# Moving rows placed 320 bytes past the weights, modulo 512, in an attention and channel-mix kernel

## The chip, the cores and the metric

The kernel runs on one core of a Trainium2 chip. The metric is the device time of one execution in microseconds. The core has a TensorE (PE; its weight loads are listed as PEld), a VectorE (DVE), a ScalarE (ACT), a GpSimd (POOL) and a SyncE (SP) that issues the DMAs. SBUF is the working memory: 128 partitions, each with its own range of byte addresses. A tile takes the same bytes of every partition. PSUM holds what TensorE accumulates.

## The reference, cut to what matters

```python
scores = scale * np.matmul(q, k.transpose(0, 1, 3, 2)) - np.log(S)     # q, k, v: 8 x 12 x 448 x 64
attn = 1.0 / (1.0 + np.exp(-scores))
x = np.matmul(attn, v)                   # then heads side by side: 8 x 448 x 768
x_prev = ...                             # x, one token earlier
xk = mu_k * x + (1.0 - mu_k) * x_prev
xr = mu_r * x + (1.0 - mu_r) * x_prev
k = np.maximum(xk @ w_k, 0.0)            # w_k: 768 x 1024
v = k * k @ w_v                          # w_v: 1024 x 768
r = 1.0 / (1.0 + np.exp(-(xr @ w_r)))    # w_r: 768 x 768
return r * v
```

The attention has no softmax, only a sigmoid. Behind it stand three products with weights: `xr @ w_r` (stage 0), `xk @ w_k` (stage 1) and `k*k @ w_v` (stage 2).

## The kernel before, in words

**Attention.** 48 pairs of heads are worked off two pairs at a time. For each of 7 strips of 64 keys, line 333 computes scores, ScalarE applies the sigmoid (line 337), and line 346 multiplies by the values. One step of either kind is four matmuls of 64x64 weights, one for each quarter of TensorE's array. Operands are plain f32 in the tiles raw, vn and pf. VectorE mixes each token with the one before it (lines 361 and 362) and the results go to DRAM as xr_d and xk_d. Beside it, VectorE converts the 64-bit weights to f32.

**Stages.** Each of the three products is a two-by-two block product done with seven block products instead of eight, over four pairs of token blocks (the first pair has blocks of 256 tokens, the others of 512). The seven left factors, sums and differences of weight blocks, lie in `slots`, one slot each. Every factor is split into a high part rounded to the type f32r and a low part, the rest, so that one product is made of three: high by high, high by low, low by high. The right factors, the activations, are fetched into ysa, ysb and other tiles (`fetch`), combined there (`minus`, line 415), and split into high and low rows by `operand` (lines 427 and 428). The split rows go into the 24 units of rra and rrb, 12 each, taken round in turn by `take`. Line 551 in `multiply` issues all matmuls of the stages: 128x128 of a slot are loaded as weights, and one row of 512 f32r columns (256 in part of the first pair of blocks) moves through the array into PSUM tile xb or yb. Each matmul has its own weight load. `evacuate` and `out_block` empty xb and yb on ScalarE and VectorE.

**Order.** All instructions of a part are put into one order by `Plan`, a list scheduler with a cost for each operation (`mm` in line 197 prices a matmul at `n * (cols / 2.4 + 13.5)` ns), priorities and data dependences. It knows no addresses. The queues of the engines then run in that order, with waits on data.

**Places in SBUF.** Tiles of a pool lie one behind the other in the order in which they are made. The pool wp stands on the left, directly above the constants; the pools on the right (apool in the attention, kp in the stages, after apool is closed) end at the top of memory, so that a longer pool begins lower. In the program of before the tiles begin at these bytes of each partition:

| Tile | first byte | modulo 512 | length |
|---|---|---|---|
| slot0 to slot6 (weights) | 16672 to 90400 | 288 | 12288 each |
| rra (moving rows) | 102688 | 288 | 24576 |
| ysa, wraw, wbit, wexpo | 127264 to 162080 | 288 | multiples of 2048 |
| rrb (moving rows) | 167712 | 288 | 24576 |
| ysb, u2, cc, wc | 192288 to 227616 | 288 | multiples of 512 |

A block of 128 weights takes 512 bytes of a partition and a row of 512 takes 2048, so all blocks of weights and all rows of the stages begin at the same byte modulo 512 as the tiles. kp already ends with an unused tile, gap1, of 48 elements or 192 bytes.

Of the kernel before, what the change touches and what calls it, by code (L numbers as in the profile page):

```python
# [8 lines left out]
F32 = mybir.dt.float32  # L9
# [89 lines left out]
def attention_then_channel_mix(  # L99
# [17 lines left out]
    P = 128  # L117
# [41 lines left out]
    def ring(pool, name, bufs, shape, dtype):  # L159
        return [pool.tile(shape, dtype, name=f"{name}{i}") for i in range(bufs)]  # L160

    wp = ctx.enter_context(tc.tile_pool(name="wp", bufs=1, side="left"))
    att = ExitStack()
    slots = [wp.tile([P, 2 * WO], F32R, name=f"slot{g}") for g in range(7)]
    RU = 2 * NJH
    rra = wp.tile([P, 2 * RU, TB], F32R, name="rra")
    ysa = wp.tile([P, RU, TB], F32, name="ysa")
    wraw = wp.tile([P, 2, WP, 2], U32, name="wraw")
# [211 lines left out]
    def take(n):  # L380
        x = rr_n[0] if rr_n[0] + n <= 4 * RU else 0
        rr_n[0] = x + n
        names = [("rra", u) if u < 2 * RU else ("rrb", u - 2 * RU) for u in range(x, x + n)]
        return [big[name][:, u] for name, u in names], names
# [112 lines left out]
    kp = ctx.enter_context(tc.tile_pool(name="kp", bufs=1, side="right", reuse_waits="tile"))  # L497
    rrb = kp.tile([P, 2 * RU, TB], F32R, name="rrb")
    ysb = kp.tile([P, RU, TB], F32, name="ysb")
    big["rrb"], big["ysb"] = rrb, ysb  # L500
    u2 = ring(kp, "u2", 4, [P, TB], F32)
    cc = ring(kp, "cc", 5, [P, TB], F32)
    wc = ring(kp, "wc", 4, [P, WC], F32)
    kp.tile([P, 48], F32, name="gap1")
    pb = ctx.enter_context(tc.tile_pool(name="pb", bufs=1, space=PSUM, reuse_waits="tile"))
    yb = ring(pb, "yb", 4, [P, TB], F32)
    xb = ring(pb, "xb", 4, [P, TB], F32)
# [198 lines left out]
```

## Time and profile before

| | |
|---|---|
| median of 3 runs | 817.62 us (817.34 to 818.55) |
| the profiled execution | 817.73 us |
| its span, first to last instruction | 815.9 us |
| granted TensorE clock, mean | 0.999 |
| TensorE busy | 810.4 us, 5259 matmuls |
| VectorE busy | 595.5 us |
| ScalarE busy | 490.3 us |

The span is what the views of the profile cover; 1.8 us of the execution lie around it. The chain of waits follows the work that ended last back to the start. In the chain in order of time, a piece of TensorE is a number of matmuls back to back; its length by its count is their spacing. The mean duration of a matmul in the groups of instructions is longer than this spacing, because matmuls overlap.

### The profile page before, as it was taken

The page shows a single profiled execution, that of the slowest core. Times are in us where ns is not written, and L with a number is a line of the kernel's source. Part 1 is how long each engine was busy: PE and PEld are TensorE (multiplying, and loading weights), DVE is VectorE, ACT ScalarE, POOL GpSimd, SP SyncE. Part 2 cuts the span into 40 slices and gives each one's busy share as a digit, 9 for nine tenths or more (in the row PEclk, how much of TensorE's full clock was granted, in tenths as well). Part 3 has the DMA queues.
Part 4 walks back from the last instruction along what each step waited for, and adds up shares of the span by engine and source line. Part 5 has one row for each costly group of instructions (what it writes and reads, how often), then busy time and mean ns, then how long its engine had stood idle before and what let it go on. Part 6 is the DMA issues. An engine that isn't in the chain of part 4 may idle for free.

```text
span 815.9 us, 14820 instructions
## 1 busy us (share of the span) xinstructions
PE 810.4 (99%) x5259; PEld 568.1 (70%) x5259; DVE 595.5 (73%) x1120; ACT 490.3 (60%) x846; POOL 10.7 (1%) x100
## 2 busy tenths in 40 slices
PE   9999999999999999999999999999999999999998
PEld 4444444444445888888888888888888888888887
DVE  1999889787666999899983624566587495494675
ACT  5776766666566756456774855878695434333442
POOL 0000000000000000000000000000000000000000
PEclk9999999999999999999999999999999999999999
DMA  9888879998954775859885531724763565554442
GB/s 303 270 301 272 275 271 346 310 369 309 301 188 155 262 243 210 286 194 308 287 263 196 194 117 51 257 74 135 272 224 107 212 217 181 174 162 155 134 139 90
DMA packets 113881, 179.77 MB, mean 220 GB/s; under 512 B 14096, under 2 KB 78608, under 8 KB 112272
## 3 DMA queue, kind: packets, MB, share of 16 engines
q1 hardware_dynamic: 113520, 178.54, 65.1%
q8 instruction: 41, 0.67, 0.3%
q10 hardware_dynamic: 288, 0.30, 0.1%
q14 instruction: 32, 0.26, 0.1%
HBM read 109.06 MB, written 69.73 MB: 219 GB/s over the span
## 4 chain that ended last, share of the span: by engine, by line
PE 97%; DVE 2%; issue 1%; ACT 0%; DMA 0%; DVEq 0%
PE xb L551 38%; PE yb L551 28%; PE sc L333 16%; PE av L346 15%; DMA raw<-in_qk 0%; DVE rrb L428 0%; DVE xo L362 0%; DVE cc L604 0%; DVE xo L361 0%; DVE ysa L415 0%; DVE ysb L415 0%; DVE rra L428 0%; DVE cc L589 0%; ACT yb L666 0%; ACT cc L601 0%
## 5 line engine op out<-in xcount | busy, mean ns | idle before, releaser
L337 ACT ACTIVATE pf<-sc 128x896 f32<-128x896 f32 x168 | 153.9, 917 | 88.2 <-PE sc L333 88.1
L551 PE MATMUL xb<-rra,slot 128*128 128x512 f32 (+1 forms) x807 | 188.1, 381 | 0.1
L551 PEld LDWEIGHTS xb<-rra,slot 128*128 128x128 f32 x807 | 147.4, 188 | 30.3 <-issue 0.7
L333 PE MATMUL sc<-raw 64*64 64x448 f32 (+1 forms) x1360 | 157.5, 535 | 0.3 <-DMA raw<-in_qk 0.2
L346 PE MATMUL av<-pf,vn 64*64 64x448 f32 x1344 | 156.2, 536 | 0.0
L551 PE MATMUL xb<-rrb,slot 128*128 128x512 f32 (+1 forms) x645 | 149.7, 378 | 0.2 <-DVE cc L604 0.2
L551 PEld LDWEIGHTS xb<-rrb,slot 128*128 128x128 f32 x645 | 116.7, 188 | 23.3 <-DVE cc L604 0.4
L551 PE MATMUL yb<-rrb,slot 128*128 128x512 f32 (+1 forms) x547 | 127.1, 380 | 0.0
L551 PE MATMUL yb<-rra,slot 128*128 128x512 f32 (+1 forms) x546 | 126.1, 378 | 0.0
L551 PEld LDWEIGHTS yb<-rrb,slot 128*128 128x128 f32 x547 | 99.5, 188 | 19.6
L551 PEld LDWEIGHTS yb<-rra,slot 128*128 128x128 f32 x546 | 98.8, 188 | 19.3
L333 PEld LDWEIGHTS sc<-raw 64*64 64x64 f32 x1360 | 53.0, 134 | 75.1 <-issue 69.5
L346 PEld LDWEIGHTS av<-pf,vn 64*64 64x64 f32 x1344 | 51.4, 133 | 74.9 <-issue 74.2
L361 DVE TENSOR_SCALAR xo<-av,omr 128x447 f32<-128x447 f32 x48 | 32.5, 677 | 43.7 <-PE av L346 43.7
L428 DVE TENSOR_TENSOR rrb<-ysa,rrb 128x512 fp32r<-128x512 f32 (+1 forms) x61 | 36.4, 633 | 32.3 <-ACT rrb L427 29.3
L601 ACT COPY u<-yb 128x512 f32<-128x512 f32 x40 | 23.3, 586 | 54.5 <-PE yb L551 54.5
L428 DVE TENSOR_TENSOR rra<-ysa,rra 128x512 fp32r<-128x512 f32 (+1 forms) x71 | 40.0, 601 | 16.8 <-ACT rra L427 10.7
L427 ACT CAST rra<-ysa 128x512 fp32r<-128x512 f32 (+1 forms) x75 | 38.6, 554 | 12.0 <-PE xb L551 5.3
L601 ACT COPY cc<-yb 128x512 f32<-128x512 f32 (+1 forms) x49 | 26.3, 542 | 26.9 <-PE yb L551 22.9
L427 ACT CAST rrb<-ysa 128x512 fp32r<-128x512 f32 (+1 forms) x61 | 33.0, 577 | 15.4 <-PE xb L551 10.9
L604 DVE TENSOR_TENSOR cc<-xb,cc 128x512 f32<-128x512 f32 x40 | 27.3, 685 | 18.6 <-ACT cc L601 18.6
L529 DVE TENSOR_TENSOR slot<-wc,slot 128x384 fp32r<-128x384 f32 x56 | 29.0, 552 | 13.5 <-ACT slot L528 13.3
(72 smaller groups left out, 744.4 us busy)
## 6 DMA issues: line engine op xcount, KB each, us to landing
raw<-in_qk SPq DMA_DIRECT2D x46, 288.0 KB, 4.0
k_d<-cc SPq DMA_DIRECT2D x48, 256.0 KB, 2.8
vn<-in_v SPq DMA_DIRECT2D x48, 224.0 KB, 4.9
xr_d<-xo SPq DMA_DIRECT2D x48, 224.0 KB, 4.0
xk_d<-xo SPq DMA_DIRECT2D x48, 224.0 KB, 3.9
r_d<-cc SPq DMA_DIRECT2D x36, 256.0 KB, 2.2
out<-cc SPq DMA_DIRECT2D x36, 256.0 KB, 3.2
raw<-in_qk SPq DMA_DIRECT2D x48, 160.0 KB, 4.2
```

Source lines behind the costliest of these rows:

```text
L333: nc.tensor.matmul(u[half[h ^ (m % 2)], m % 2, q], x[half[h], c], x[half[h], KQ + q.start:KQ + q.stop], start=True, stop=True)
L337: op(ACT, act(2 * S), at, lambda: nc.scalar.activation(f, u[:, :, :S], AF.Sigmoid, bias=NEG_LOG_S, scale=SCALE), [("sc", t % 2)], [("pf", ...
L346: nc.tensor.matmul(av[bank(m)][half[r ^ (m % 2)], :S], vn[m % RAW][half[r], j, :], pf[t % PFB][half[r], m % 2, :], start=j == 0, stop=j == ...
L361: op(DVE, dve(S, ptr=True), at, lambda y=y, om=om: nc.vector.tensor_scalar_mul(y[:, 1:], x[:, :S - 1], om[:, j:j + 1]), [X, ("om", key)], [Y])
L427: op(ACT, act(w, True), at, lambda t=t: nc.scalar.copy(hi[t], y[:, t, :w]), [Y[t]], [H[t]])
L428: op(DVE, dve(w), at, lambda t=t: nc.vector.tensor_sub(lo[t], y[:, t, :w], hi[t]), [Y[t], H[t]], [L[t]])
L529: op(DVE, dve(WC), at, lambda h_=h_, l_=l_, w=w: nc.vector.tensor_sub(l_, w, h_), [W, K + (h, "hi")], [K + (h, "lo")])
L551: nc.tensor.matmul(o, a[:, c], b, start=first and e == 0, stop=e == len(terms) - 1, skip_group_check=True)
L601: op(ACT, act(src.shape[-1]), at, lambda: nc.scalar.copy(dst, src), R, [D_])
L604: op(DVE, dve(a.shape[-1]), at, lambda: nc.vector.tensor_add(dst, a, b), R, [D_])
```

## The change

An unused tile of 80 f32 elements, 320 bytes, is put between the slots and rra, and the unused tile at the end of kp grows from 48 elements to 96, from 192 bytes to 384.

```diff
     slots = [wp.tile([P, 2 * WO], F32R, name=f"slot{g}") for g in range(7)]
     RU = 2 * NJH
+    wp.tile([P, 80], F32, name="gap0")
     rra = wp.tile([P, 2 * RU, TB], F32R, name="rra")
     ysa = wp.tile([P, RU, TB], F32, name="ysa")
     wraw = wp.tile([P, 2, WP, 2], U32, name="wraw")
...
     wc = ring(kp, "wc", 4, [P, WC], F32)
-    kp.tile([P, 48], F32, name="gap1")
+    kp.tile([P, 96], F32, name="gap1")
     pb = ctx.enter_context(tc.tile_pool(name="pb", bufs=1, space=PSUM, reuse_waits="tile"))
```

rra, and behind it ysa, wraw, wbit and wexpo, begin 320 bytes higher. kp is 192 bytes longer, so rrb and the other tiles of kp begin 192 bytes lower. The slots and the tiles of the attention stay in place.

## The prediction

> **What bounds the kernel now.** I read four views: busy time by engine, the chain of waits, the chain in order of time, and the stages' busy windows. First the page.
>
> ```profile
> span 815.9 us, 14820 instructions
> PE 810.4 (99%) x5259; PEld 568.1 (70%) x5259; DVE 595.5 (73%) x1120; ACT 490.3 (60%) x846; POOL 10.7 (1%) x100
> PE 97%; DVE 2%; issue 1%; ACT 0%; DMA 0%; DVEq 0%
> PE xb L551 38%; PE yb L551 28%; PE sc L333 16%; PE av L346 15%; DMA raw<-in_qk 0%; DVE rrb L428 0%; DVE xo L362 0%; DVE cc L604 0%; DVE xo L361 0%; DVE ysa L415 0%; DVE ysb L415 0%; DVE rra L428 0%; DVE cc L589 0%; ACT yb L666 0%; ACT cc L601 0%
> ```
>
> TensorE alone makes 97% of the chain. Two thirds of it (38% + 28%) are the matmuls of line 551, whose moving rows lie in rra and rrb: the instructions that the padding touches. Next, what one of them costs. In the chain in order of time the columns are start, length and work; the pieces have no wait between them, so length by count is the spacing of consecutive matmuls.
>
> ```profile
> 249.83 0.75 PE av L346 x8
> 250.58 0.75 PE sc L333 x8
> 251.33 0.75 PE av L346 x8
> 252.08 0.75 PE sc L333 x8
> ...
> 524.50 12.59 PE xb L551 x72
> 537.08 8.40 PE yb L551 x48
> ...
> 594.70 8.16 PE xb L551 x36
> 602.86 8.16 PE yb L551 x36
> ```
>
> A 36-piece of full rows gives 8.16 / 36 = **226.7 ns for 512 columns**. The pieces at 524.50 belong to the first pair of blocks, where every product takes as many 256-column as 512-column matmuls: 12.59 / 72 = 174.9 ns on average, so a 256-column one takes 2 x 174.9 - 226.7 = **123.1 ns**.
>
> The attention shows how fast columns can stream. A piece of 8 records is one step of four matmuls of 64x64, each in its own quarter of the array and recorded twice. From 249.83 to 252.08 three pieces take 2.25 us, or 750 ns each, so a quarter gets two records of 448 columns in 750 ns: 375 ns a record, 0.837 ns a column. A plain-f32 record there is nearly twice as dear by the column as an f32r one in the stages (226.7 / 512 = 0.443). If it streams its columns twice, one pass takes 0.4185 ns a column, and 512 columns take 214.3 ns, 256 take 107.1. An **excess of 12.4 ns** per 512-column matmul and 16.0 per 256-column one is left in the stages. (The kernel's planner, line 197, prices the same thing at 13.5 ns.) That excess is all the change can act on.
>
> How many carry it, and what else is near its limit, by shape and by window:
>
> ```profile
> L551 PE MATMUL xb<-rra,slot 128*128 128x512 f32 x744 | 182.9, 390 | 0.1
> L551 PE MATMUL xb<-rrb,slot 128*128 128x512 f32 x576 | 144.0, 390 | 0.2 <-DVE cc L604 0.2
> L551 PE MATMUL yb<-rrb,slot 128*128 128x512 f32 x497 | 122.5, 390 | 0.0
> L551 PE MATMUL yb<-rra,slot 128*128 128x512 f32 x489 | 121.7, 390 | 0.0
> L551 PE MATMUL xb<-rrb,slot 128*128 128x256 f32 x69 | 11.4, 280 | 0.0
> L551 PE MATMUL xb<-rra,slot 128*128 128x256 f32 x63 | 10.7, 281 | 0.0
> L551 PE MATMUL yb<-rra,slot 128*128 128x256 f32 x57 | 9.5, 281 | 0.0
> L551 PE MATMUL yb<-rrb,slot 128*128 128x256 f32 x50 | 7.9, 281 | 0.0
> ```
>
> ```profile
> 280.00:420.00 140.00, 140.00 (x622) 116.03 (x621) 131.15 (x252) 87.86 (x172) 0.00 (x0) 1.00 0.73 247
> 420.00:782.00 362.00, 362.00 (x1638) 301.12 (x1637) 225.97 (x403) 207.85 (x409) 0.00 (x0) 1.00 0.52 172
> ```
>
> The 512-column groups hold 744 + 576 + 497 + 489 = 2306, the 256-column ones 69 + 63 + 57 + 50 = 239. In the window rows (window, its length, then PE, PEld, DVE, ACT, POOL, clock, DMA) PE is busy the whole time at clock 1.00, so neither the clock nor a feeding engine holds the cadence; but from 280 to 420 VectorE has only 140 - 131.15 = 8.9 us to spare.
>
> **The change part by part.** Two tiles that nobody uses are sized anew; no instruction is added, removed or reordered, and the planner reads no address.
>
> *Moving rows.* Weights stay at byte 288 modulo 512. rra goes from 288 to 608, which is 96, and rrb from 167712 to 167520, also 96. So every product of line 551 reads its moving row 320 bytes past the weights (modulo 512), where before the two offsets were equal. All slices within the slots begin at multiples of 512 bytes, all rows at multiples of 2048, so no matmul of the stages is an exception. Each comes with a load of weights that runs beside the row of the matmul before it:
>
> ```profile
> L551 PEld LDWEIGHTS xb<-rra,slot 128*128 128x128 f32 x807 | 147.4, 188 | 30.3 <-issue 0.7 <-ACT cc L601 0.3
> L333 PEld LDWEIGHTS sc<-raw 64*64 64x64 f32 x1360 | 53.0, 134 | 75.1 <-issue 69.5 <-ACT slot L300 2.9 <-ACT pf L337 1.1
> ```
>
> A load lasts 188 ns inside a spacing of 226.7, so 38.7 ns are left over: the load does not set the spacing by its length, and would have to grow by that before it did. What it may do is disturb the row that streams beside it, and the excess is the room for that. No two offsets stand side by side in the stages before, so the price of the new offset is unknown and is bounded from both sides. **Lower end:** the whole excess goes, 12.4 x 2306 + 16.0 x 239 = 28.6 + 3.8 = 32.4 us. In the first window that would take 622 x 12.4 = 7.7 us, which still fits into VectorE's 8.9. **Upper end:** as much again is added, 32.4 us; a load could not be in the way much more often than that without its own 188 ns having shown it. **Taken:** a quarter of the excess goes. The ground is geometry, not a row: a row of 2048 bytes passes four stretches of 512, and with equal offsets its first stretch starts in the load's own place; with 320 between them, no stretch starts there. A quarter of 12.4 is 3.1 ns: 3.1 x 2306 + 4.0 x 239 = 7.1 + 1.0 = 8.1 us off. I lean to a gain rather than a loss because an equal start is where two streams coincide at once in every matmul, and because a cost of 12 ns in the stages stands beside none that can be seen in the attention.
>
> *The rule against it.* The row: 226.7 ns where 214.3 would do, with a 188-ns load alongside. The Trainium skill, "TensorE: Matmul & The Clock Gate", section "Step-by-step: what each phase is for", states that TensorE has two independent SBUF read ports, one for the moving operand and one for the weights, and that loading the next weights takes no bandwidth from the running matmul; "SBUF — State Buffer", "Who interferes with whom", adds that PE waits on nobody. By that rule an offset changes nothing and the sum is 817.7; it is the first rival below. The trace neither confirms nor refutes it, since it has one offset only.
>
> *The other tiles.* ysa, wraw, wbit, wexpo, ysb, u2, cc and wc also move from 288 to 96 modulo 512. Their VectorE and ScalarE work lies under TensorE except at the seam between attention and stages:
>
> ```profile
> 258.13 0.74 DVE xo L361 x2
> ...
> 264.54 1.43 DVE rrb L428 x4
> ...
> 268.38 1.00 ACT yb L666 x2
> ...
> 276.13 2.38 PE xb L551 x12
> ```
>
> ```profile
> L428 DVE TENSOR_TENSOR rrb<-ysa,rrb 128x512 fp32r<-128x512 f32 (+1 forms) x61 | 36.4, 633 | 32.3 <-ACT rrb L427 29.3
> ...
> L428 DVE TENSOR_TENSOR rra<-ysa,rra 128x512 fp32r<-128x512 f32 (+1 forms) x71 | 40.0, 601 | 16.8 <-ACT rra L427 10.7
> L427 ACT CAST rra<-ysa 128x512 fp32r<-128x512 f32 (+1 forms) x75 | 38.6, 554 | 12.0 <-PE xb L551 5.3
> ...
> L427 ACT CAST rrb<-ysa 128x512 fp32r<-128x512 f32 (+1 forms) x61 | 33.0, 577 | 15.4 <-PE xb L551 10.9
> ```
>
> From 258.13 to 276.13 other engines lead for part of 18.0 us. I cost this at nothing: the DVE subtractions into rra and rrb were at one offset, and no row shows the offset to matter to them. As a bound, groups of like work at one offset differ by 4 to 5% (subtractions 601 ns against 633, casts 554 against 577), and 5% of 18.0 is 0.9 us either way. The right-hand pool starts 192 bytes lower, over the same attention tiles but for two or three edges, and its waits fall in the same stretch. Attention tiles do not move: that part stays as it is.
>
> *Sum.* The profiled execution took 817.73 us, 0.1 above the median of 817.62; 815.9 are span, 1.8 lie around it. 815.9 - 8.1 + 1.8 = **809.6 us**.
>
> **The rivals.**
>
> 1. *Nothing happens.* The excess is a fixed price of changing 128x128 weights. For it: 8.16 us per 36 in both pieces at 594.70 and 602.86, whatever the other engines and the DMA do, and an attention whose operands lie 0 and 256 bytes apart in turns (rows at 512 in raw, weights at multiples of 256) and whose pieces are all 0.75 us. Against it: the excess is not one number (12.4 beside 16.0), and the attention changes weights nearly free. Time: 817.7, with the seam 816.8 to 818.6. That the padding is dropped would give the same; little speaks for it, since the 192-byte pad of before does shift rrb.
>
> 2. *Slower: the row runs into the load.* From the rows above, a load takes 188 - 134 = 54 ns for 64 more columns, 0.84 ns a column or 4.7 bytes per ns; a row goes at 2048 / 214.3 = 9.6. With equal offsets the row is ahead from the start and gains 4.9 bytes per ns; it needs 512 / 4.9 = 104 ns to lap the load, whose 128 columns take 108: they part at once and meet only at the end. With 320 bytes between them the row has 192 to make up, 192 / 4.9 = 39 ns, and meets the load in the middle. If the memory serves one of them at a time there, before had the favourable offset. It decides as soon as one meeting delays the row at all, as nothing behind TensorE could hide it. Price: a quarter of the excess more, 8.1 us, gives 825.8; doubled it is 850.1. For it: 226.7 has no irregular member in the full blocks. Against it: equal offsets should then have shown no excess.
>
> 3. *The whole excess is collisions and goes.* 817.7 - 32.4 = 785.3, with VectorE then at 131.15 of 132.3 us between 280 and 420. Against it: it would take an offset at which the streams never meet, and at 4.9 bytes per ns the two pass each other once in 104 ns anyway.
>
> **How the numbers follow.** Forecast (some of the excess gone, 801 to 816): 0.35. Nearly all gone (785 to 801): 0.08. No change, by the fixed price or the two ports: 0.25. Slower: 0.32. The bound of faster and slower is 0.2%, 1.6 us, about what measurements of this kernel can tell from no change. So faster 0.43, same 0.25, slower 0.32. The predicted time is the forecast's, 809.6; its own range is 801 to 816. The range over all cases runs from 797, which leaves out most of rival 3, to 832, which leaves out the slower case where its price passes 14 / 2545 = 5.6 ns per matmul.
>
> **What would show it.** The pieces of 36 in the chain: 8.05 us (223.6 ns) by the forecast, 8.16 by rival 1, 8.27 by rival 2, 7.71 by rival 3. rra and rrb must show the same spacing, as both have the new offset; if only one does, one pad is not where it should be. The pieces of 72 become 36 x 223.6 + 36 x 119.1 = 12.34 us. The attention's pieces must stay at 0.75 and the seam at 18.0. The prediction is wrong if the 36-piece does not move, if it grows, or if VectorE becomes the releaser of matmuls between 280 and 420.

## The result, and the profile after

The changed kernel is a little slower: **822.15 us** (821.13 to 822.97) against 817.7 before, a ratio of 1.0051 with a 95% interval of 1.0041 to 1.006. That is 4.5 us. Its profiled execution took 822.2 us.

The page of the changed kernel, then its chain in order of time (start, length, work; lines of code are one higher than before):

```profile
span 820.4 us, 14820 instructions
PE 814.1 (99%) x5259; PEld 567.6 (69%) x5259; DVE 596.4 (73%) x1120; ACT 490.4 (60%) x846; POOL 10.0 (1%) x100
```

```profile
254.15 0.75 PE sc L334 x8
...
256.41 2.27 PE av L347 x24
...
276.68 2.37 PE xb L552 x12
...
527.41 12.48 PE xb L552 x72
...
597.73 8.24 PE xb L552 x36
...
812.16 2.78 PE yb L552 x16
```

TensorE is still the whole chain, and the attention's pieces still take 0.75 us. What moved is the spacing in the stages. A piece of 36 full rows takes 8.24 us where it took 8.16: 8.24 / 36 = 228.9 ns, **2.2 ns more for each 512-column matmul**. The pieces of 72 in the first pair of blocks, where 512-column and 256-column matmuls alternate, went the other way: 12.48 for 12.59, or 1.6 ns less for each matmul (173.3 for 174.9). It is not the 256-column matmuls that gained. In these pieces, for the same 24 matmuls of 512 columns, before and then after (the last two numbers ahead of the second bar are the busy time in us and the mean duration in ns):

```profile
L551 PE MATMUL yb<-rra,slot 128*128 128x512 f32 x24 | 6.9, 395 | 0.0
```

```profile
L552 PE MATMUL yb<-rra,slot 128*128 128x512 f32 x24 | 6.8, 391 | 0.0
```

Their mean duration fell by 4 ns; that of the 256-column ones beside them fell by 2, from 281 to 279. The spacing says it more plainly. From the start of each single record to the start of the next, averaged over all pieces of the first pair in stage 1, a 512-column matmul took 232.2 ns before and 228.7 after, a 256-column one 117.7 and 118.0. So beside 256-column matmuls, equal places were not the good case: the same 512 columns that take 226.7 ns among full rows took 232.2 there. Over the counts in the prediction the change is worth (2306 - 239) x 2.2 - 2 x 239 x 1.6 = 4.55 - 0.76 = 3.8 us.

The trace agrees with this sum. The stretch of the chain that the stages' matmuls hold ran from 276.68 to 814.94 after, 538.3 us. (Their first few run earlier, in the seam behind the attention, where other engines lead.) Before, it began at 276.13, and its last piece was

```profile
807.61 2.82 PE yb L551 x16
```

so it ran to 810.43, for 534.3 us. So 4.0 of the 4.5 us lie in the stages. The last piece of the attention begins 0.57 us later than before (256.41 against 255.84); the seam behind it is the same, 20.3 us from there to the piece at 276.68, and so is the tail behind the last matmul. That half microsecond is no more than the scatter of the early part: in the kernel of the first experiment below, whose attention is the same, it is 0.44 the other way (255.40), and in the other kernels of the experiments that ran at full clock the piece begins between 255.4 and 256.5.

### The profile page after: what moved, and what is told of

The parts are those of the page before. It is cut to its first block, busy times and chain, and to the rows that moved or that the text cites. A ratio compares the mean times of both kernels' runs of the same rounds, so it can differ in the third digit from the quotient of the medians.

```text
span 820.4 us, 14820 instructions
## 1 busy us (share of the span) xinstructions
PE 814.1 (99%) x5259; PEld 567.6 (69%) x5259; DVE 596.4 (73%) x1120; ACT 490.4 (60%) x846; POOL 10.0 (1%) x100
## 4 chain that ended last, share of the span: by engine, by line
PE 93%; DVE 3%; DMA 2%; issue 1%; ACT 1%; SPq 0%; DVEq 0%; ACTq 0%
PE xb L552 38%; PE yb L552 28%; PE sc L334 14%; PE av L347 14%; DMA wraw<-in_moe_w_r 1%; DMA ysa<-xr_d 1%; DMA raw<-in_qk 0%; DVE xo L363 0%; DVE xo L362 0%; DVE rrb L429 0%; DVE wbit L227 0%; ACT pf L338 0%; DVE cc L605 0%; DVE wbit L228 0%; DVE wbit L256 0%
## 5 line engine op out<-in xcount | busy, mean ns | idle before, releaser
L552 PEld LDWEIGHTS yb<-rrb,slot 128*128 128x128 f32 x547 | 99.6, 188 | 20.3
L552 PEld LDWEIGHTS yb<-rra,slot 128*128 128x128 f32 x546 | 98.7, 188 | 20.3
```

What stands on the lines that cost most here:

```text
L552: nc.tensor.matmul(o, a[:, c], b, start=first and e == 0, stop=e == len(terms) - 1, skip_group_check=True)
```

## The experiments

The theory after the result: **the cadence of the stages hangs on the distance between the moving rows and the weights**, and equal offsets are the better case. The first rivals: that the absolute place of the rows does it, or that the other tiles do, which moved along. After these were out, the question was which distances are good, and which reads have to agree.

Spacings are read in the timeline of TensorE: its groups are runs of matmuls on one tile, and the start of a group to the start of the next, by its count, is the spacing. Where rows of rra and rrb alternate, the second of two groups on one tile is taken, away from the change of tile.

**Everything moved together.**

```diff
+    wp.tile([P, 80], F32, name="gap2")
     slots = [wp.tile([P, 2 * WO], F32R, name=f"slot{g}") for g in range(7)]
...
-    kp.tile([P, 48], F32, name="gap1")
+    kp.tile([P, 96], F32, name="gap1")
```

> Everything is moved together: an unused tile of 320 bytes stands before the slots, so weights, rra and all tiles behind them lie at 96 modulo 512, and the right-hand pool is 192 bytes lower, also at 96. Rows and weights are at equal offsets again, but every tile of the stages lies where the change put it. If the distance between row and weights sets the cadence: pieces of 36 at 8.16 us, time 817.7. If the absolute place of the rows or the move of the other tiles (ysa, wbit, cc and so on) did it: 8.24 us and 822.2.

Measured: 818.0 us, ratio to before 1.0001 (0.9991 to 1.001). Its chain in order of time:

```profile
255.40 2.27 PE av L347 x24
...
594.27 8.16 PE xb L552 x36
```

8.16 us again. Every tile of the stages lies where the change put it (rra at byte 103008, rrb at 167520), and nothing is lost. So the place as such and the other tiles are out; the distance from the weights counts.

**One half of the change: rra alone.**

```diff
     RU = 2 * NJH
+    wp.tile([P, 80], F32, name="gap0")
     rra = wp.tile([P, 2 * RU, TB], F32R, name="rra")
```

> One half of the change alone: rra is 320 bytes past the weights, rrb keeps the offset of the weights. If each row's own distance counts: matmuls on rra at 228.9 ns, on rrb at 226.7, and the time in between, about 820.1 (rra carries 1233 of 2306 full matmuls, so 53% of 4.5 us is 2.4). If the slowing has another cause that is shared by both tiles, both show one spacing.

Measured: 822.4 us, ratio 1.0057 (1.0042 to 1.0072). The timeline of TensorE in this kernel:

```profile
493.47 8.32 PE L552 MATMUL yb<-rrb,slot 128*128 128x512 f32 x36
501.63 8.42 PE L552 MATMUL yb<-rra,slot 128*128 128x512 f32 x36
509.89 8.40 PE L552 MATMUL xb<-rra,slot 128*128 128x512 f32 x36
518.13 8.37 PE L552 MATMUL yb<-rrb,slot 128*128 128x512 f32 x36
526.34 3.99 PE L552 MATMUL xb<-rrb,slot 128*128 128x512 f32 x21
```

The spacings are as expected: rrb from 493.47 to 501.63, 8.16 us or 226.7 ns; rra from 509.89 to 518.13, 8.24 or 228.9. The time is not: half of the change costs as much as the whole. Two things show why. The first group after a change of tile is slower: rrb from 518.13 to 526.34 takes 8.21, 0.05 more than the settled 8.16. In the single records the first ten spacings or so after the change lie between 224 and 236 ns, then they settle at 226 to 227. The kernel changes tiles at every second product in stages 0 and 1. In stage 2 every third product takes its high rows from rra and its low rows from rrb, so that one row in three comes from the other tile, and there the cost is larger. One such product in its chain:

```profile
654.76 8.39 PE xb L552 x36
```

8.39 / 36 = 233.1 ns, where the same product takes 8.16 before and 8.24 with the whole change. The records show seven such products, 252 matmuls at 233.4 ns; over 226.7 that is 252 x 6.7 = 1.7 of the 4.7 us. So a matmul's spacing does not depend on its own reads alone, and alternating between two distances can cost more than either distance kept throughout.

**Which distances are good.** The next kernels put rra and rrb at two distances each, by two numbers:

```diff
+    wp.tile([P, 8], F32, name="gap0")        # 8, 128, 32, 24, 56 elements: 32, 512, 128, 96, 224 bytes
     rra = wp.tile([P, 2 * RU, TB], F32R, name="rra")
...
-    kp.tile([P, 48], F32, name="gap1")
+    kp.tile([P, 112], F32, name="gap1")      # 112, 32, none, 8, 104 elements: 256, 64, 192, 160, 288 bytes
```

> rra lies 32 bytes past the weights and rrb 256 bytes past. If the cost grows with the distance from an equal start: rra between 226.7 and 228.9 ns, rrb about 228.9. If it is a matter of a period shorter than 512 (64, 128 or 256), 256 bytes is as good as none, 226.7, and 32 bytes differs most.

Its timeline, with rra 32 and rrb 256 bytes past the weights:

```profile
495.23 8.32 PE L552 MATMUL yb<-rrb,slot 128*128 128x512 f32 x36
503.39 8.57 PE L552 MATMUL yb<-rra,slot 128*128 128x512 f32 x36
511.79 8.56 PE L552 MATMUL xb<-rra,slot 128*128 128x512 f32 x36
520.19 8.36 PE L552 MATMUL yb<-rrb,slot 128*128 128x512 f32 x36
```

At 256 bytes the spacing is 8.16 / 36 = 226.7 ns, as at none; at 32 it is 8.40 / 36 = 233.3. A distance of 32 bytes is thus three times as dear as the 320 of the change (6.7 against 2.2 ns), as the second expectation, a period shorter than 512, has it for 256 bytes. The execution took 825.67 us.

A kernel with 512 and 64 bytes was run twice. The first execution ran at a granted clock of 0.557 throughout and took 1394 us, so its times say nothing. What was expected of it:

> rra is moved by 512 bytes and rrb lies 64 bytes past the weights. If only the distance modulo 512 counts, matmuls on rra stay at 226.7 ns; if a longer modulus counts they move. For 64 bytes: if two streams that start in one place cost most, below 226.7; if equal offsets are the favourable case, above 226.7 and up to 228.9.

> The kernel of the run at half clock again: rra 512 bytes away, rrb 64 bytes past the weights. The steady spacing away from changes of tile is read. If only the distance modulo 512 or a divisor of it counts: rra 226.7 ns. If the pattern repeats every 256 bytes (as 0 and 256 are alike so far), 64 must do what 320 does: rrb 228.9. If it does not repeat before 512: rrb anything between 226.7 and 233.4, the values at 0 and 32.

```profile
493.19 8.40 PE L552 MATMUL yb<-rrb,slot 128*128 128x512 f32 x36
501.43 8.37 PE L552 MATMUL yb<-rra,slot 128*128 128x512 f32 x36
509.64 8.32 PE L552 MATMUL xb<-rra,slot 128*128 128x512 f32 x36
517.80 8.42 PE L552 MATMUL yb<-rrb,slot 128*128 128x512 f32 x36
```

The second execution, at full clock: rrb at 64 bytes 8.24 (228.9 ns, as at 320), rra at 512 bytes 8.16 (226.7). 822.71 us. With that the **period is 256 bytes**: 0, 256 and 512 are alike, and so are 64 and 320.

> rra 128 and rrb 192 bytes past the weights. If the pattern repeats every 128 bytes: rra 226.7 and rrb as at 320 and 64, 228.9. If it repeats every 256: both are new, and if the cost falls steadily from 32 bytes on (233.4 at 32, 228.9 at 64) they lie at 226.7 to 228. If there is an offset better than equal ones, it shows below 226.7; then the whole excess is not a fixed price.

```profile
497.31 8.56 PE L551 MATMUL yb<-rrb,slot 128*128 128x512 f32 x36
505.71 8.53 PE L551 MATMUL yb<-rra,slot 128*128 128x512 f32 x36
514.08 8.52 PE L551 MATMUL xb<-rra,slot 128*128 128x512 f32 x36
522.44 7.86 PE L551 MATMUL yb<-rrb,slot 128*128 128x512 f32 x33
```

At 192 bytes 8.40 (233.3 ns), at 128 bytes 8.36 (232.2). Neither expectation held: 128 is not as good as none, and the cost doesn't fall steadily with distance. 829.85 us.

> rra 96 and rrb 160 bytes past the weights, both odd multiples of 32. If odd multiples of 32 are the bad ones whatever the rest (a period of 64): both 233.4 ns. If the cost falls with the distance from an equal start: below 228.9 at both.

```profile
498.00 8.59 PE L552 MATMUL yb<-rrb,slot 128*128 128x512 f32 x36
506.43 8.57 PE L552 MATMUL yb<-rra,slot 128*128 128x512 f32 x36
514.84 8.56 PE L552 MATMUL xb<-rra,slot 128*128 128x512 f32 x36
523.24 6.95 PE L552 MATMUL yb<-rrb,slot 128*128 128x512 f32 x29
```

At 160 bytes 8.43 (234.2 ns), at 96 bytes 8.40 (233.3). 832.41 us. These odd multiples of 32 are as dear as expected for a period of 64, but 192 (233.3) and 64 (228.9) differ, so 64 is not the period.

> rra 224 and rrb 288 bytes past the weights: 32 short of 256 and 32 past it. If the pattern repeats every 256 bytes, rrb does what 32 bytes does, 233.4 ns. If only the distance to an equal offset counts, not its sign, rra shows 233.4 as well; if it matters who is ahead, rra stays below.

```profile
498.44 8.56 PE L552 MATMUL yb<-rrb,slot 128*128 128x512 f32 x36
506.84 8.55 PE L552 MATMUL yb<-rra,slot 128*128 128x512 f32 x36
515.23 8.56 PE L552 MATMUL xb<-rra,slot 128*128 128x512 f32 x36
523.63 6.70 PE L552 MATMUL yb<-rrb,slot 128*128 128x512 f32 x28
```

At 288 bytes 8.40 (from 498.44 to 506.84), at 224 bytes 8.40 (from 515.23 to 523.63), 233.3 ns both. 288 does what 32 does, which fits the period of 256, and at 32 bytes the side makes no difference. 832.22 us.

Finer steps were made with slices, since all tiles of these kernels begin at multiples of 32 bytes:

```diff
-    rra = wp.tile([P, 2 * RU, TB], F32R, name="rra")
+    rra = wp.tile([P, 2 * RU * TB + 128], F32R, name="rra")
...
-        return [big[name][:, u] for name, u in names], names
+        at = [u * TB + (4 if name == "rra" else 60) for name, u in names]
+        return [big[name][:, a:a + TB] for (name, _), a in zip(names, at)], names
```

rrb is widened in the same way.

> Rows are placed 16 bytes past the weights in rra and 240 in rrb, 16 short of 256, by slicing wider tiles; both tiles begin where they did. If the cost has its steps at 32 bytes or more: rra at 226.7 as for equal offsets. If it is sharper: rra between 226.7 and 233.3 or beyond, and rrb at 233.3 to 234 like 224 and 160. Below 226.7 in either, a better offset than the equal one exists.

```profile
370.07 12.91 PE L552 MATMUL xb<-rrb,slot 128*128 128x512 f32 x54
382.81 6.41 PE L552 MATMUL xb<-rra,slot 128*128 128x512 f32 x27
389.06 6.42 PE L552 MATMUL yb<-rra,slot 128*128 128x512 f32 x27
...
498.49 8.56 PE L552 MATMUL yb<-rrb,slot 128*128 128x512 f32 x36
506.89 8.50 PE L552 MATMUL yb<-rra,slot 128*128 128x512 f32 x36
```

16 bytes past the weights: from 382.81 to 389.06, 6.25 / 27 = 231.5 ns. 16 short of 256, two values stand in one trace: from 370.07 to 382.81, in stage 0, 12.74 / 54 = 235.9, the dearest of all; from 498.49 to 506.89, in stage 1, 8.40 / 36 = 233.3. (In the single records stage 1 shows both, each held over whole groups.) So the distance alone does not fix the spacing there; what else does was not tried. 830.28 us. For full rows, then, equal places are a sharp optimum: 16 bytes to either side cost more than the 64 of the change. All distances, modulo 256, in ns per 512-column matmul among full rows; most of them come from a single execution of one kernel:

| 0 | 16 | 32 | 64 | 96 | 128 | 160 | 192 | 224 | 240 |
|---|---|---|---|---|---|---|---|---|---|
| 226.7 | 231.5 | 233.3 | 228.9 | 233.3 | 232.2 | 234.2 | 233.3 | 233.3 | 233.3 and 235.9 |

The change took 64 modulo 256, the second best. None of them beats equal offsets for full rows, and none of these kernels beats the one before. The mixed pieces of 72 have another order: in the kernels of this section they take 12.53 to 12.63 us, at equal places 12.59, and the change's 12.48 is the least.

**Do the loads have a part in it?**

```diff
+    wp.tile([P, 8], F32, name="gap0")
     rra = wp.tile([P, 2 * RU, TB], F32R, name="rra")
...
+    for b in xb + yb:
+        nc.vector.memset(b[P // 2:], 0.0)
...
-                c = slice(t * w + i * P, t * w + (i + 1) * P)
-                nc.tensor.matmul(o, a[:, c], b,
+                c = slice(t * w + i * P, t * w + i * P + P // 2)
+                nc.tensor.matmul(o[:P // 2], a[:, c], b,
```

> Half the work is left out: each matmul of the stages loads 64 of its 128 columns of weights and fills half of its PSUM tile (the other half is set to zero once). Rows are streamed as before, 512 columns each. rra lies 32 bytes past the weights, rrb is level with them. If the excess comes from the load's reads beside the row, half a load brings half of it: level rows from 226.7 to about 220 ns, rows 32 bytes off from 233.3 to about 223. If it is a fixed price of changing weights: 226.7 stays, and only the 6.7 of the offset may shrink. If loads have no part in it: both stay, 226.7 and 233.3.

```profile
501.18 8.44 PE L554 MATMUL yb<-rrb,slot 128*64 128x512 f32 x36
509.46 8.47 PE L554 MATMUL yb<-rra,slot 128*64 128x512 f32 x36
517.76 8.47 PE L554 MATMUL xb<-rra,slot 128*64 128x512 f32 x36
526.08 4.31 PE L554 MATMUL yb<-rrb,slot 128*64 128x512 f32 x18
```

```profile
L554 PEld LDWEIGHTS xb<-rra,slot 128*64 128x64 f32 x807 | 108.6, 136 | 78.5 <-issue 7.7
```

The loads became shorter (136 ns for 188), and both spacings moved, in opposite ways: level rows from 226.7 to 8.28 / 36 = 230.0 ns, rows 32 bytes off from 233.3 to 8.32 / 36 = 231.1. None of the three expectations fits. Rows and places were the same, so a fixed price of changing weights is unlikely, and so is a cost in proportion to the load: with less loading the level case was dearer. The output of a matmul was halved too, so the load is not alone in having changed, and this run does not settle the question.

**Which reads have to agree?** High and low parts got places of their own:

```diff
-    slots = [wp.tile([P, 2 * WO], F32R, name=f"slot{g}") for g in range(7)]
+    slots = [wp.tile([P, WO], F32R, name=f"slot{g}") for g in range(7)]
+    wp.tile([P, 8], F32, name="gap2")
+    slots_lo = [wp.tile([P, WO], F32R, name=f"slot_lo{g}") for g in range(7)]
+    wp.tile([P, 120], F32, name="gap3")
...
-        return slots[g][:, :n], slots[g][:, n:2 * n], ("slot", g)
+        at = 120 if stage == 0 else 0
+        return slots[g][:, :n], slots_lo[g][:, at:at + n], ("slot", g)
...
-        return [big[name][:, u] for name, u in names], names
+        at = [u * TB + 128 * (u >= RU) + 8 * (lo_from is not None and k >= lo_from) for k, (_, u) in enumerate(names)]
+        return [big[name][:, a:a + TB] for (name, _), a in zip(names, at)], names
```

`lo_from` is the number of high rows in stages 0 and 1 and absent in stage 2; rra and rrb are 256 elements longer.

> High and low parts get places of their own. Low rows lie 32 bytes further than high rows in stages 0 and 1; the low weights lie level with the high ones in stage 0 and 32 bytes further in stages 1 and 2. All else as before. A matmul streams its row while the weights of the next matmul are loaded. In a triple (high weights with high row, high weights with low row, low weights with high row) the loads beside them are high, low, high. If what counts is the row against the load beside it: stage 1 has equal places in all three and stays at 226.7 ns; in stage 0 the low rows run beside a load 32 bytes off and in stage 2 the loads of low weights are 32 off, a third of the matmuls each, 226.7 + 6.67 / 3 = 228.9 if thirds add. If what counts is the row against its own weights: in stage 1 two of three are off (low row with high weights, low weights with high row), 231.1 if thirds add; stages 0 and 2 have one in three, 228.9. If only the place of the row on its own counts: stage 2 at 226.7, stage 1 at 228.9.

Its chain, one piece of each stage:

```profile
369.34 18.76 PE xb L556 x81
...
471.64 25.08 PE xb L556 x108
...
619.14 25.19 PE xb L556 x108
```

Stage 0: 18.76 / 81 = 231.6 ns; stage 1: 25.08 / 108 = 232.2; stage 2: 25.19 / 108 = 233.2. Time 830.87 us. Stage 1 is not at 226.7, so agreement of a row with the load of the next weights is not enough. Thirds do not add either: in stages 0 and 2, where one matmul in three is off its place, the excess over 226.7 is 4.9 and 6.5 ns, three quarters and nearly all of the 6.6 that rows cost which all lie 32 bytes off.

The same layout with 256 bytes in place of 32 (64 elements for 8, and gaps of 64 and 64):

> The same layout as in the run with high and low parts apart, with 256 bytes in place of 32: low rows 256 bytes further than high rows in stages 0 and 1, low weights level in stage 0 and 256 bytes further in stages 1 and 2. If a distance of 256 is as good as none for every pair of reads, whoever meets whom, all three stages stay at 226.7 ns and the time at 817.7; the 231.7 to 233.1 of that run then come from its 32 bytes. If splitting the tiles or mixing two places within a triple costs something by itself, it shows here above 226.7.

```profile
367.07 18.36 PE xb L556 x81
...
491.51 16.32 PE yb L556 x72
...
611.57 24.48 PE xb L556 x108
```

18.36 / 81 (stage 0), 16.32 / 72 (stage 1) and 24.48 / 108 (stage 2) are all 226.7 ns; 818.26 us. The layout costs nothing that can be seen, and the period of 256 holds for every pair of reads that it puts 256 bytes apart. Last, two other pairings, with the low weights 32 bytes on and one row of each triple read 32 bytes later (so that its columns are not the right ones):

```diff
-            terms = [(t, a, b, bank) for t in range(n) for a, b in ((whi, u[t]), (whi, u[n + t]), (wlo, u[t]))]
+            x = [later[r] for r in R[:n]] if stage < 2 else u[:n]
+            terms = [(t, a, b, bank) for t in range(n) for a, b in ((whi, u[t]), (whi, u[n + t]), (wlo, x[t]))]
```

In the second kernel `x[t]` stands in the first place of the triple.

> Low weights lie 32 bytes further than high ones in all stages. In stages 0 and 1 the third matmul of each triple (low weights) reads its row 32 bytes later than it lies, so 8 columns on (its columns are then not the right ones, the work is the same). Every row of these stages is then at the place of its own weights, while the row against the load of the next weights is off in two of three. If row and own weights must agree: stages 0 and 1 at 226.7 ns, stage 2, where rows are not shifted, above as before (233.1). If a change of place from one read to the next costs in itself: stages 0 and 1 between 231 and 234.

> As the other, but the first matmul of each triple reads its row 32 bytes later. Every row of stages 0 and 1 is then at the place of the weights of the matmul after the next, while it is off its own weights in two of three. If the reads that meet are a row and the load two matmuls ahead: stages 0 and 1 at 226.7 ns. Otherwise 231 to 234, and if both runs show that, no single pairing decides and every change of place costs.

The chain of the first, then of the second:

```profile
369.61 18.90 PE xb L558 x81
...
472.51 25.20 PE xb L558 x108
```

```profile
370.11 18.82 PE xb L558 x81
...
472.53 25.08 PE xb L558 x108
```

233.3 ns in both stages of the first (831.4 us), 232.3 and 232.2 in the second (830.86 us). None of the three pairings brings 226.7 back by itself: a row with the next load, with its own weights, or with the load two matmuls ahead. As expected for that case, the runs show only this much: among full rows 226.7 was seen only where the reads that follow one another, rows and loads together, keep one place modulo 256 and the last change of place lies some ten matmuls back; one read in three that doesn't is enough to lose it.

## Why the prediction was right or wrong

It was wrong in its sign: 809.6 was forecast, 822.15 came, inside the range but outside the forecast's own 801 to 816.

*What held.* The view of the bound held: TensorE's spacing in the stages is where 4.0 of the 4.5 us lie, and nothing else became a bound. Of the 140 us from 280 to 420 VectorE now has 9.9 to spare (window, its length, PE, PEld, DVE):

```profile
280.00:420.00 140.00, 140.00 (x616) 115.03 (x616) 130.15 (x249) 86.91 (x169) 0.00 (x0) 1.00 0.73 245
```

The attention stayed at 0.75 us a piece. Both tiles show the same spacing, 8.24 us for 36 rows. The cost of nothing for the other tiles was right: the run with everything moved together gives 1.0001. The 0.5 us at the early part lies inside the 0.9 set aside, though not at the seam.

*The step that failed* is "Taken: a quarter of the excess goes", and with it the ground given, that an equal start is where two streams coincide. Of the 12.4 ns of excess nothing went; 2.2 were added. For full rows equal places are the best of all that were tried, and 16 bytes away the spacing is already at 231.5. The excess at equal places was read as room for a gain, and that was the deeper fault. Its 12.4 ns come from the assumption that the attention streams every column twice and loses nothing, so "none that can be seen in the attention" was put in, not found. No run shows 214.3 ns; the least settled spacing among full rows is 226.7. And no row showed a part of the excess hanging on place. Whether the 12.4 ns are a loss at all, and of what, remains open; the run with half loads speaks against a fixed price, as both spacings changed.

*Rival 2* had the sign, with a price of 3.1 ns where 2.2 were measured, and 825.8 us where 822.15 were. Its mechanism doesn't fit the runs. By its speeds a row 32 bytes ahead of the load parts from it at once and comes round to it after 480 bytes, 480 / 4.9 = 98 ns, nearly as late as the 104 of an equal start, so 32 should have been nearly as good as none; it costs 233.3. With the period of 256 it would be 46 ns for 52, near each other again. And by it a halved load should have eased every case; level rows got 3.3 ns dearer.

*Rival 1* and the rule behind it fell. The Trainium skill ("TensorE: Matmul & The Clock Gate", "Step-by-step: what each phase is for") has two independent read ports, by which place should not matter. The traces differ: with the same instructions the spacing of full rows goes from 226.7 to 235.9 ns with the distance, and moving rows and weights together undoes the loss of the change. What rival 1 took from the attention, that offsets of 0 and 256 bytes do alike, is true of the stages too, but there 256 is a full period, so it was no evidence that offsets don't matter.

*The 256-column matmuls* were sized at 123.1 ns, with a gain of 4.0. Both go back to a misreading: the working took 226.7 ns for the 512-column matmuls beside them, which by the starts of the records took 232.2, so the 256-column ones took 117.7, and they stayed there (118.0). It was the 512-column ones beside them that gained 3.5 ns, some 0.8 us in all. With that, the second excess is not 16.0 but 10.6 ns, and 17.9 for the 512-column ones beside them. Why the mixed sequence gains where full rows lose was not tried. A slip without weight: 14 / 2545 is 5.5, not 5.6.

*Still open:* which of TensorE's reads disturb each other. The kernels with mixed places exclude each of the three pairings that were tried as the only one, but since a disturbance lasts over several matmuls, they can't say which pairing starts it. Open as well are the two values at 240 bytes and the mixed 512- and 256-column sequence.

## What to carry to other kernels

Where f32r matmuls of 512 columns follow each other with a new load of weights each, put moving rows and weights at the same byte modulo 256 in the partition: at other distances this kernel's full rows cost 1 to 4% more. Don't mix places in one sequence: with the change's distance on two rows of three and none on the third, a matmul cost 233.4 ns, with the change's distance on all rows 228.9. Other shapes have to be tried by themselves; where 512 and 256 columns alternate, this kernel did slightly better at the change's distance (173.3 ns for 174.9). Before a mean over two kinds of instruction is split by an assumed price for one, read the starts of the single records. Before a difference in cost is taken for room, look for a row in which it varies with the thing to be changed. A pad that shifts one of two tiles should be tried together with a pad that shifts both, which separates distance from place in one run.

## What the runs showed of the hardware that was not expected

- The spacing of 512-column matmuls among full rows depends on the distance between moving rows and weights in SBUF, and as far as tried it repeats after 256 bytes: 226.7 ns at 0, 256 and 512, 228.9 at 64 and 320, 233.3 at 32 and 288. At 240 bytes 233.3 and 235.9 were seen in one trace.
- A change from one distance to another is felt over some ten matmuls: the first 36 after it take 8.21 us instead of 8.16. Alternating within every three matmuls, between none and 320 bytes, keeps the spacing at 233.4.
- Among 256-column matmuls, 512-column ones at equal places take 232.2 ns, and 228.7 at 320 bytes.
- With half the weights loaded and half the output, level matmuls were slower, 230.0 ns for 226.7.
